# A two-stage kernel on one core: the normalized rows of its second part, turned by VectorE and a trip through DRAM

## The chip, the core and the metric

The kernel runs on one core of a Trainium2 chip. The core has a matrix engine (TensorE, in the profile PE for its matmuls and PEld for its weight loads), VectorE (DVE), ScalarE (ACT), GpSimd (POOL) and SyncE (SP), which here issues the DMAs. Sixteen DMA engines move data between DRAM and the on-chip memory SBUF; matmuls write to PSUM, which has eight banks. The metric is the device time of one execution in microseconds (us). All arithmetic is in float32.

## The reference

Two stages. The first is linear attention with random features; the second mixes its output with a Fourier transform and applies a two-layer network.

```python
def phi(x):
    proj = np.einsum('bhsd,md->bhsm', x, omega)
    sq = np.sum(x * x, axis=-1, keepdims=True) / 2.0
    h = proj - sq
    h = h - np.max(h, axis=-1, keepdims=True)
    return np.exp(h) / np.sqrt(m)
q_p, k_p = (phi(q_s), phi(k_s))
kv = np.einsum('bhsm,bhsd->bhmd', k_p, v)
z = np.sum(k_p, axis=2)
num = np.einsum('bhsm,bhmd->bhsd', q_p, kv)
den = np.einsum('bhsm,bhm->bhs', q_p, z)[..., None] + 1e-06
...
X = np.fft.fft(x, axis=1)
X = np.fft.fft(X, axis=2)
mixed = np.real(X).astype(np.float32)
u = x + mixed
mu = np.mean(u, axis=-1, keepdims=True)
var = np.mean((u - mu) ** 2, axis=-1, keepdims=True)
un = (u - mu) / np.sqrt(var + 1e-06)
ch = np.maximum(un @ w_ch1, 0.0) @ w_ch2
return (u + ch).astype(np.float32)
```

Shapes: q, k and v are 8 x 8 x 576 x 64, so u has 8 x 576 = 4608 rows of 512 numbers; w_ch1 is 512 x 2048 and w_ch2 is 2048 x 512.

## The kernel before

**Two parts.** The first part (to about 424 us) does the attention, the Fourier mixing, which leaves u in a DRAM tensor `us`, and the network for the first 512 rows in four plain tiles of 128. The second part does the network for the other 4096 rows in eight blocks of 512 (`TB`), numbered j = 0 to 7. The change is in the second part.

**One block.** The rows are normalized and turned: `norm_of` (line 966) loads 128 rows of u, VectorE takes mean and variance (`bn_stats`, `bn_aggr`), GpSimd raises the variance to the power -1/2, VectorE subtracts and scales (line 981), TensorE turns the four 128 x 128 squares by transposing them against a unit matrix (line 985), and ScalarE copies the turned tile from PSUM to SBUF (line 989). A matmul needs the contracted index on the partitions, which is why the rows must be turned. `block_norms` (line 1097) does this for the four tiles of a block and leaves two turned halves `un[0]` and `un[1]` of 256 rows each, and forms four sums of their quarters on VectorE (line 1113).

Both matrix products are done by a scheme of the Strassen kind: seven products of half-size instead of eight. `first_of(j, fc)` (line 1240) makes one pair of 128 hidden columns by seven *first products* (line 1252): its moving operand is a quarter of `un` or a sum `tt`, 256 rows wide. ScalarE saves partial results (`s`, line 1266), VectorE adds them with the relu (`hid`, line 1238), GpSimd makes sums of the results (`hs`, line 1319). There are eight such pairs in a block. `product_of(j, i, cells)` (line 1373) makes one of the seven *second products*, each split again in seven parts (*leaves*) of four matmuls (line 1432): 49 leaves a block. Each leaf multiplies by its own 256 KB of prepared second-layer weights, `wl`, which `loads_w2` (line 1327) loads from DRAM ahead of use into a ring of `NWL` buffers. `second_of` (line 1497) loads the rows of u for the residual (`ur`) and stores the results.

**What sets the order.** The order of the instructions on every engine is fixed when the kernel is built. The parts of the work are Python generators that yield a `Step` for each operation, with its engine, an estimated duration, the events it waits for and the buffers it takes and gives. `Listing.run` (line 184) keeps a clock for each engine and always lists the step that can start first by those estimates (`bias` shifts that). So a change of steps changes the order of everything around it. On the chip each engine runs its list in order and waits by semaphores; a waiting instruction holds up all that stands behind it on its engine. SyncE's queue is such a list too. The second part is one call of `Listing.run` (line 1539) over `late_norms`, `halves`, `loads_w2` and `weight_sums`.

Four buffers named `slab` hold `un[0]`, `un[1]` and the sums. There is one set, so the next block's rows can only be turned into place when the first products of this block are done; in the kernel before, the norms of block j + 1 therefore lie among the second products of block j.

Of the kernel before, what the change touches and what calls it, by code (L numbers as in the profile page):

```python
# [17 lines left out]
F32 = mybir.dt.float32  # L18
# [17 lines left out]
PE, ACT, DVE, POOL, SP, NONE = "pe", "act", "dve", "pool", "sp", "none"  # L36
# [244 lines left out]
def kernel(  # L281
# [10 lines left out]
    nc = tc.nc  # L292
# [15 lines left out]
    P = 128  # L308
# [10 lines left out]
    TP = 128  # L319
    NPLAIN = 4  # L320
    TB = 512
    NWL, NSUM = 13, 3
    NTB = (B * S - NPLAIN * TP) // TB
    HF, HT, HM = NFC // 2, TB // 2, DM // 2
    D2, F2 = NDC // 2, DFF // 2
# [621 lines left out]
    def load_rows(dst, t):  # L947
        nc.sync.dma_start(dst, us[P * t : P * (t + 1), :])
# [12 lines left out]
    def events_of(tt):  # L961
        return tuple(sorted({("us", r // S) for t in tt for r in (P * t, P * t + P - 1)}))

    unTs = {}

    def norm_of(j, t, i, pool, dst):

        yield Step(SP, 0.42, 3.0, take=("u",), kb=256)
        u = pool.tile([P, DM], F32, name="u", tag="u", bufs=2)
        load_rows(u[:], t)  # L970
        st = small.tile([P, 6], F32, name="st", tag="st")
        mv = small.tile([P, 2], F32, name="mv", tag="mv")
        rstd = small.tile([P, 1], F32, name="rstd", tag="rstd")
        yield Step(DVE, 1.12 if pool is mlpp else 1.01, bias=-0.23)
        nc.vector.bn_stats(out=st[:], in_=u[:])
        nc.vector.bn_aggr(out=mv[:], in_=st[:])
        nc.vector.tensor_scalar(rstd[:], mv[:, 1:2], 1e-6, None, op0=ALU.add)  # L977
        yield Step(POOL, 1.05 if pool is mlpp else 0.85, port=True, bias=-0.18)
        nc.gpsimd.tensor_tensor(rstd[:], rstd[:], mhalf[:], op=ALU.pow)  # L979
        yield Step(DVE, 0.455, port=True)  # L980
        nc.vector.tensor_scalar(u[:], u[:], mv[:, 0:1], rstd[:], op0=ALU.subtract, op1=ALU.mult)
        yield Step(PE, 0.437, take=("bank",), give=("u",))
        b, tp = got()
        for dc in range(NDC):
            nc.tensor.transpose(  # L985
                tp[:, 128 * dc : 128 * dc + 128], u[:, 128 * dc : 128 * dc + 128], ident[:]
            )
        yield Step(ACT, 0.5, give=(b,), makes=("unT", j, i), bias=0.33)
        nc.scalar.activation(
            out=dst,  # L990
            in_=tp.rearrange("p (d t) -> p d t", d=NDC),
            func=AF.Copy,
        )

# [102 lines left out]
    def block_norms(j, pool):  # L1097
        t0 = (NPLAIN * TP + TB * j) // 128
        yield Step(NONE, take=("slab",) * 4, after=events_of(range(t0, t0 + TB // 128)) + ("converted",))
        un = unTs[j] = [slabs.tile([128, NDC, HT], F32, name="unT2", tag="slab") for _ in range(2)]  # L1100
        tt = [slabs.tile([128, 2, D2, HT], F32, name="tt", tag="slab") for _ in range(2)]
        tts[j] = tt[0][:, 0], tt[0][:, 1], tt[1][:, 0]
        for i in range(TB // 128):
            h, k = divmod(i, HT // 128)
            dst = un[h][:, :, 128 * k : 128 * k + 128]
            yield Fork(norm_of(j, t0 + i, i, pool, dst))
        yield Step(NONE, after=tuple(("unT", j, i) for i in range(TB // 128)), bias=1.54)
        ops = sums_right(
            un[0][:, 0:D2], un[1][:, 0:D2], un[0][:, D2:NDC], un[1][:, D2:NDC], *tts[j]
        )  # L1110
        for i, (o, l, r, op) in enumerate(ops):
            yield Step(DVE, 0.6, makes=("tt", j) if i == 3 else None, port=True, bias=-0.49)
            nc.vector.tensor_tensor(out=o, in0=l, in1=r, op=op)
# [89 lines left out]
    def pairs(start):  # L1203
# [24 lines left out]
    late = ctx.enter_context(tc.tile_pool(name="late", bufs=1))  # L1228
    listing.clock = SECOND
    listing.buffers = {k: [0.0] * n for k, n in dict(  # L1230
        slab=0, u=2, ht=NFC, ur=3, s=6, set=3, wl=NWL, sums=NSUM, part=4,
    ).items()}
    w1s += [late.tile([128, 3, D2, GW], F32, name=f"w1s{g}") for g in range(1, 4)]
    hid = late.tile([128, NFC, TB], F32, name="hid")
# [5 lines left out]
    def first_of(j, fc):  # L1240

        un, tt = unTs[j], tts[j]
        f, f2 = (slice(128 * c, 128 * c + 128) for c in (fc, fc + HF))
        g = 128 * fc // GW
        fg = slice(f.start - GW * g, f.stop - GW * g)
        me = ("first", j, fc)
        lo, hi = hid[:, fc], hid[:, HF + fc]
        t1, t2 = slice(0, HT), slice(HT, TB)

        def product(ps, left, right, start):  # L1250
            for dc in range(D2):
                nc.tensor.matmul(  # L1252
                    ps[:, 0:HT],
                    lhsT=left(dc),
                    rhs=right(dc),
                    start=start and dc == 0,
                    stop=(dc == D2 - 1),
                    skip_group_check=True,
                )

        saved = {}

        def save(name, ps):
            yield Step(ACT, 0.37, 0.1, take=("s",), makes=(me, name), bias=-2.15)
            s = late.tile([128, HT], F32, name="s", tag="s", bufs=6)
            nc.scalar.activation(out=s[:], in_=ps[:, 0:HT], func=AF.Copy)  # L1266
            saved[name] = s

        def added(name, o, ps, with_, give, after=()):
            yield Step(DVE, 0.42, 0.1, after=((me, with_),) + after, makes=(me, name), give=give, bias=1.96)  # L1270
            relu_sum(o, ps[:, 0:HT], saved[with_][:])

        mm = 8 * HT / 1193.0 / 2
        yield Step(PE, mm, after=(("tt", j), ("w1s", g)), take=("bank",), bias=0.37)
        xb, x = got()
        product(x, lambda d: w1[:, d, f], lambda d: un[0][:, d], True)
        yield Fork(save("p1", x))
        yield Step(PE, mm, take=("bank",))
        zb, z = got()
        product(z, lambda d: w1s[g][:, 0, d, fg], lambda d: tt[0][:, d], True)  # L1280
        yield Fork(save("p5", z))
        yield Step(PE, mm, after=((me, "p1"),))
        product(x, lambda d: w1s[g][:, 1, d, fg], lambda d: tt[1][:, d], False)
        yield Fork(save("u2", x))
        yield Step(PE, mm, after=((me, "p5"),), makes=(me, "z"))
        product(z, lambda d: w1s[g][:, 2, d, fg], lambda d: un[1][:, D2 + d], False)
        yield Fork(added("c12", lo[:, t2], z, "u2", (zb, "s"), ((me, "z"),)))
        yield Step(PE, mm, after=((me, "u2"),), makes=(me, "u3"))
        product(
            x,  # L1290
            lambda d: w1s[0][:, 3, d, fg] if g == 0 else w1[:, d, f2],
            lambda d: un[1][:, d],
            False,
        )
        yield Fork(added("c22", hi[:, t2], x, "p5", ("s",), ((me, "u3"),)))
        yield Step(PE, mm, take=("bank",), makes=(me, "y"))
        yb, y = got()
        product(y, lambda d: w1[:, D2 + d, f], lambda d: un[0][:, D2 + d], True)
        yield Fork(added("c11", lo[:, t1], y, "p1", (yb, "s"), ((me, "y"),)))
        last = ("slab",) * 4 if fc == HF - 1 else ()  # L1300
        yield Step(PE, mm, after=((me, "c22"),), give=("set",) + last)
        product(x, lambda d: w1[:, D2 + d, f2], lambda d: tt[2][:, d], False)
        yield Step(ACT, 0.37, 0.1, give=(xb,), makes=(me, "c21"), bias=0.73)
        nc.scalar.activation(out=hi[:, t1], in_=x[:, 0:HT], func=AF.Relu)

        yield Step(
            POOL,
            0.75,
            after=tuple((me, c) for c in ("c11", "c12", "c22"))
            + ((("second", j - 1, ORDER[-1]), "read"),) * (j > 0),  # L1310
            port=True,
        )
        ops = sums_left(
            lo[:, t1], hi[:, t1], lo[:, t2], hi[:, t2], *(hs[:, fc, i] for i in range(3))
        )
        for i, (o, l, r, op) in enumerate(ops):
            if i:
                yield Step(POOL, 0.75, makes=("hs", j, fc) if i == 3 else None, port=True, bias=0.56)
            nc.gpsimd.tensor_tensor(out=o, in0=l, in1=r, op=op)  # L1319
# [204 lines left out]
    def halves():  # L1524
        for j in range(NTB):
            for fc in range(HF):
                yield Step(NONE, take=("set", "ht", "ht"))
                yield Fork(first_of(j, fc))
            cells = {}
            yield Fork(second_of(j, cells))  # L1530
            for i in ORDER:
                yield Step(NONE, take=("set",))
                yield Fork(product_of(j, i, cells))

    def late_norms():
        for j in range(1, NTB):
            yield from block_norms(j, late)

    listing.run([late_norms(), halves(), loads_w2(), weight_sums((1, 2, 3))])


# [28 lines left out]
```

## Time and profile before

| what | value |
|---|---|
| time, median of 3 runs | 1177.97 us (1177.2, 1177.97, 1179.43) |
| span of the profiled execution, first to last instruction | 1180.9 us |
| granted TensorE clock, mean | 0.999 |
| busy PE, DVE, ACT, POOL | 1164.9, 722.6, 452.4, 412.9 us |
| L1252, first products: four groups by operands | 1792 passes of 256 columns |
| L1432, second products: three groups by operands | 3136 passes of 128 columns |
| L985, turning of rows | 144 transposes, 112 of them in the second part |
| moved by DMA | 205.67 MB, mean 174 GB/s |

The profiled execution has no time of its own beside the span; the span is 2.9 us above the median of the runs. A line of the profile names an engine, an operation, the tiles that are written and read, and how often. Each float32 matmul of the program shows as two passes; a transpose shows as one. The mean duration of a pass in the groups overlaps with its neighbours; the pace is read from the chain of waits.

### The profile page before, as it was taken

Reading aid. Unit: us, or ns where it says so; the run is one execution under the profiler, and the core shown is the slowest. Engines: PE = TensorE matmul, PEld = TensorE weight load, DVE = VectorE, ACT = ScalarE, POOL = GpSimd, SP = SyncE. Lnnn points to the kernel's source line nnn. Section 1 sums busy time; section 2 is a strip of 40 time slices with the busy share of each in tenths; the row PEclk is TensorE's granted clock in tenths of the full one; section 3 lists DMA queues with packets and bytes.
Section 4 is the critical chain, followed back from the end, with each engine's and each line's share of the span. In section 5 each row is a group of like instructions: output and inputs, shape, how many; then the busy total and the mean of one; then the engine's idle time right before and its main releaser. Section 6 shows DMA issues by size and latency. Waiting matters only on the chain.

```text
span 1180.9 us, 31428 instructions
## 1 busy us (share of the span) xinstructions
PE 1164.9 (99%) x12549; PEld 1044.6 (88%) x12549; DVE 722.6 (61%) x1552; ACT 452.4 (38%) x1513; POOL 412.9 (35%) x489
## 2 busy tenths in 40 slices
PE   8999999999999999999999999999999999999998
PEld 7878888779787878998998998998999899899898
DVE  7989999976677642762662572473374275266255
ACT  7987888866343212222222222222222222222211
POOL 2443544455462124214314304223322421431421
PEclk9999999999999999999999999999999999999999
DMA  8855756666662260861771582384295095177155
GB/s 238 245 165 173 244 174 180 200 197 178 188 203 91 88 224 10 291 194 52 240 242 64 174 286 85 118 293 134 63 304 179 10 301 193 44 245 236 63 169 189
DMA packets 144705, 205.67 MB, mean 174 GB/s; under 512 B 49072, under 2 KB 58544, under 8 KB 144560
## 3 DMA queue, kind: packets, MB, share of 16 engines
q1 hardware_dynamic: 144064, 203.41, 53.9%
q8 instruction: 99, 1.62, 0.6%
q14 instruction: 46, 0.38, 0.1%
q10 hardware_dynamic: 496, 0.26, 0.1%
HBM read 171.90 MB, written 35.91 MB: 176 GB/s over the span
## 4 chain that ended last, share of the span: by engine, by line
PE 90%; DVE 4%; DMA 3%; ACT 1%; issue 1%; SPq 1%; DVEq 0%; ACTq 0%
PE banks L1252 33%; PE banks L1432 30%; PE banks L1045 5%; PE banks L606 4%; PE banks L1068 4%; PE banks L512 4%; PE banks L640 2%; PE banks L687 2%; DMA kq<-in_q_dram 2%; PE banks L985 2%; PE banks L849 1%; PE banks L799 1%; DVE nmx L549 1%; PE banks L809 1%; DMA kq<-in_k_dram 1%
## 5 line engine op out<-in xcount | busy, mean ns | idle before, releaser
L1238 DVE CUSTOM_DVE_ANT_0 hid<-banks,s 128x256 f32<-128x256 f32 x192 | 79.6, 423 | 255.4 <-PE banks L1252 250.5
L1432 PE MATMUL banks<-wl,sums 128*128 128x128 f32 x1792 | 217.3, 275 | 0.0
L1432 PEld LDWEIGHTS banks<-wl,sums 128*128 128x128 f32 x1792 | 208.8, 192 | 0.4
L566 ACT ACTIVATE e<-banks,nmx 128x128 f32<-128x128 f32 x576 | 164.7, 428 | 24.5 <-DVE nmx L549 24.0
L1266 ACT ACTIVATE s<-banks 128x256 f32<-128x256 f32 x192 | 73.7, 384 | 261.1 <-PE banks L1252 261.1
L1252 PE MATMUL banks<-unT,w 128*128 128x256 f32 x704 | 167.5, 379 | 0.0
L1252 PEld LDWEIGHTS banks<-unT,w 128*128 128x128 f32 x704 | 132.7, 190 | 17.9 <-issue 0.5
L1407 ACT ACTIVATE s<-banks 128x128 f32<-128x128 f32 x168 | 46.6, 278 | 242.3 <-PE banks L1432 195.7
L1252 PE MATMUL banks<-tt,w1s 128*128 128x256 f32 x512 | 126.2, 379 | 0.0
L1319 POOL TENSOR_TENSOR hs<-hid 128x256 f32<-128x256 f32 x64 | 46.4, 725 | 207.9 <-DVE hid L1238 178.9
L1252 PEld LDWEIGHTS banks<-tt,w1s 128*128 128x128 f32 x512 | 97.3, 190 | 13.2
L1412 DVE TENSOR_TENSOR part<-banks,s 128x128 f32<-128x128 f32 x168 | 48.8, 291 | 88.6 <-PE banks L1432 88.4
L549 DVE TENSOR_REDUCE nmx<-banks 128x8 f32<-128x1024 f32 (+1 forms) x96 | 89.3, 951 | 21.6 <-PE banks L606 16.8
L1432 PE MATMUL banks<-wl,hid 128*128 128x128 f32 x768 | 97.6, 275 | 0.0
L1432 PEld LDWEIGHTS banks<-wl,hid 128*128 128x128 f32 x768 | 93.5, 192 | 1.2
L1319 POOL TENSOR_TENSOR hs<-hid,hs 128x256 f32<-128x256 f32 x64 | 46.6, 728 | 119.8 <-issue 94.9
L606 PE MATMUL banks<-om,kqT 64*64 64x128 f32 (+1 forms) x2088 | 80.2, 278 | 2.2 <-ACT kv L656 0.9
L1252 PE MATMUL banks<-unT,w1s 128*128 128x256 f32 x320 | 80.7, 379 | 0.0
L606 PEld LDWEIGHTS banks<-om,kqT 64*64 64x64 f32 (+1 forms) x2088 | 65.4, 140 | 13.8 <-issue 4.4
L979 POOL TENSOR_TENSOR rstd<-rstd,mhalf 128x1 f32<-128x1 f32 x36 | 24.8, 689 | 149.6 <-DVE rstd L977 148.6
L1432 PE MATMUL banks<-wl,hs 128*128 128x128 f32 x576 | 74.9, 275 | 0.4 <-DVE part L1412 0.4
L1432 PEld LDWEIGHTS banks<-wl,hs 128*128 128x128 f32 x576 | 70.0, 192 | 0.9 <-DVE part L1412 0.6
(128 smaller groups left out, 1951.6 us busy)
## 6 DMA issues: line engine op xcount, KB each, us to landing
wl<-w2l SPq DMA_DIRECT2D x392, 256.0 KB, 3.6
raw<-in_moe_w_ch_dram SPq DMA_DIRECT2D x32, 512.0 KB, 5.0
kq<-in_k_dram SPq DMA_DIRECT2D x32, 288.0 KB, 4.4
kq<-in_q_dram SPq DMA_DIRECT2D x32, 288.0 KB, 4.8
vd<-in_v_dram SPq DMA_DIRECT2D x32, 288.0 KB, 4.9
u<-us SPq DMA_DIRECT2D x36, 256.0 KB, 3.9
ur<-us SPq DMA_DIRECT2D x36, 256.0 KB, 3.8
out_dram<-ur SPq DMA_DIRECT2D x34, 256.0 KB, 2.4
```

What stands on the lines that cost most here:

```text
L512: nc.tensor.transpose(ps[:, (j - j0) * 128 : (j - j0 + 1) * 128], src(j), ident[:])
L549: nc.vector.tensor_reduce(nmx[:, :, 0:num], pps[:, :, 0 : MF * num].rearrange("p b (c m) -> p b c m", m=MF), axis=AX.X, op=ALU.max, negate ...
L566: nc.scalar.activation(out=e[:, c + (i if num == 1 else 0), :], in_=pps[:, i, MF * c : MF * c + MF], func=AF.Exp, bias=nmx[:, i, c : c + 1],)
L606: nc.tensor.matmul(pps[cols, c, MF * m : MF * m + MF], lhsT=kqT[rows, j, cols], rhs=om2[rows, :],)
L1045: nc.tensor.matmul(hp[:, 0:TP], lhsT=w1[:, dc, 128 * fc : 128 * fc + 128], rhs=unTs[key][:, dc, :], start=(dc == 0), stop=(dc == NDC - 1),)
L1068: nc.tensor.matmul(yp[:, 0:DM], lhsT=hs[fc][:, 128 * i : 128 * i + 128], rhs=w2[:, fc, :], start=(fc == 0), stop=(fc == NFC - 1),)
L1238: nc.vector._custom_dve(TENSOR_ADD_SAT, out=o, in0=ps, in1=sb, s0=FMAX, s1=0.0)
L1252: nc.tensor.matmul(ps[:, 0:HT], lhsT=left(dc), rhs=right(dc), start=start and dc == 0, stop=(dc == D2 - 1), skip_group_check=True,)
L1266: nc.scalar.activation(out=s[:], in_=ps[:, 0:HT], func=AF.Copy)
L1319: nc.gpsimd.tensor_tensor(out=o, in0=l, in1=r, op=op)
L1412: nc.vector.tensor_tensor(out=part[:, t, 128 * m : 128 * m + 128], in0=ps[:, 0:128], in1=saved[with_][:], op=ALU.add,)
L1432: nc.tensor.matmul(ps[:, 0:128], lhsT=left[:, f], rhs=wls[j, i, n][:, f], start=start and f == 0, stop=(f == 3), skip_group_check=True,)
```

## The change

In blocks 1 to 7 of the second part the rows are no longer turned by TensorE and ScalarE.

- `by_blocks`: VectorE transposes each 32 x 32 square of a normalized tile of 128 rows in place of its position, all 16 squares in one instruction, into a tile `turn` (one buffer). SyncE writes that to a DRAM tensor `turned`, 256 KB in runs of 512 bytes.
- `fetched`: for each half block SyncE reads it back in four DMAs of 128 KB, each into 32 partitions of `un`, so that the squares land where the turned tile needs them. Eight DMAs a block.
- `normed` and `late_turns`: load, statistics, normalization, turn and write are a stream of their own, listed first. It may start for block j once the first pair of columns of block j - 1 has been made; the fetch alone waits for the `slab` buffers.
- The 128 rows of a tile are now taken from two adjacent tiles in alternating groups of 32 (`rows[block[1]]`), so that a run read back is 1 KB.
- `un` and the sums have the layout [row group of 32][piece of 128 features][32 rows] instead of [piece][256 rows]. A first product's moving operand is therefore eight runs of 32 numbers, 128 apart (64 apart in the sums). Block 0 is still turned by TensorE, and ScalarE writes it in the new layout.
- The ring of weights has 12 buffers instead of 13.

```diff
-    NWL, NSUM = 13, 3
+    NWL, NSUM = 12, 3
...
+    Q = 32
+    turned = {}
+
+    def by_blocks(j, i, pool, u, h, k):
+        yield Step(DVE, 0.69, take=("turn",), give=("u",), makes=("turn", j, i))
+        w = pool.tile([P, 4, NDC, Q], F32, name="turn", tag="turn", bufs=1)
+        nc.vector.transpose(
+            out=w[:].rearrange("p g d q -> p d g q"),
+            in_=u[:].rearrange("p (d g q) -> p d g q", d=NDC, g=4),
+        )
+        if (j, h) not in turned:
+            turned[j, h] = dram.tile([P, 4, 2, NDC * Q], F32, name=f"turned{j}_{h}")
+        t = turned[j, h]
+        yield Step(SP, 0.42, 2.6, after=(("turn", j, i),), makes=("turned", j, i), give=("turn",), kb=165)
+        nc.sync.dma_start(t[:, :, k], w[:].rearrange("p g d q -> p g (d q)"))
+
+    def fetched(j, h, dst):
+        yield Step(
+            SP, 1.7, 3.0, after=(("turned", j, 2 * h), ("turned", j, 2 * h + 1)),
+            makes=("unT", j, h), kb=330,
+        )
+        for g in range(4):
+            nc.sync.dma_start(
+                dst[Q * g : Q * g + Q].rearrange("q (b k) d t -> q b (k d t)", k=2),
+                turned[j, h][:, g].rearrange("(b q) k n -> q b (k n)", q=Q),
+            )
+
+    def normed(j, pool):
+        t0 = (NPLAIN * TP + TB * j) // 128
+        yield Step(NONE, after=events_of(range(t0, t0 + TB // 128)) + ((("first", j - 1, 0), "z"),))
+        for i in range(TB // 128):
+            h, k = divmod(i, HT // 128)
+            yield from norm_of(j, t0 + 2 * h, i, pool, None, (h, k))
+
+    def norm_of(j, t, i, pool, dst, block=None):
...
-        load_rows(u[:], t)
+        if block:
+            rows = us[P * t : P * (t + 2), :].rearrange("(b k q) d -> k b q d", k=2, q=Q)
+            nc.sync.dma_start(u[:], rows[block[1]])
+        else:
+            load_rows(u[:], t)
...
+        if block:
+            yield from by_blocks(j, i, pool, u, *block)
+            return
         yield Step(PE, 0.437, take=("bank",), give=("u",))
...
-        un = unTs[j] = [slabs.tile([128, NDC, HT], F32, name="unT2", tag="slab") for _ in range(2)]
-        tt = [slabs.tile([128, 2, D2, HT], F32, name="tt", tag="slab") for _ in range(2)]
+        un = unTs[j] = [slabs.tile([128, HT // Q, NDC, Q], F32, name="unT2", tag="slab") for _ in range(2)]
+        tt = [slabs.tile([128, 2, HT // Q, D2, Q], F32, name="tt", tag="slab") for _ in range(2)]
         tts[j] = tt[0][:, 0], tt[0][:, 1], tt[1][:, 0]
         for i in range(TB // 128):
             h, k = divmod(i, HT // 128)
-            dst = un[h][:, :, 128 * k : 128 * k + 128]
-            yield Fork(norm_of(j, t0 + i, i, pool, dst))
+            if pool is mlpp:
+                dst = un[h][:, 4 * k : 4 * k + 4].rearrange("p g d q -> p d g q")
+                yield Fork(norm_of(j, t0 + i, i, pool, dst))
+            elif not k:
+                yield Fork(fetched(j, h, un[h]))
...
-                    ps[:, 0:HT],
+                    ps[:, 0:HT].rearrange("f (b q) -> f b q", q=Q),
...
-        product(x, lambda d: w1[:, d, f], lambda d: un[0][:, d], True)
+        product(x, lambda d: w1[:, d, f], lambda d: un[0][:, :, d], True)
...
+    def late_turns():
+        for j in range(1, NTB):
+            yield from normed(j, late)
 
-    listing.run([late_norms(), halves(), loads_w2(), weight_sums((1, 2, 3))])
+    listing.run([late_turns(), late_norms(), halves(), loads_w2(), weight_sums((1, 2, 3))])
```

The numbers in the steps are the listing's own estimates; they set the order, not the time.

More of the change, by code (lines that the diff above doesn't have):

```diff
@@ L964 @@
     unTs = {}
-    def norm_of(j, t, i, pool, dst):
+    Q = 32
[29 more added lines that the diff above has]
+    def norm_of(j, t, i, pool, dst, block=None):
         yield Step(SP, 0.42, 3.0, take=("u",), kb=256)
         u = pool.tile([P, DM], F32, name="u", tag="u", bufs=2)
-        load_rows(u[:], t)
+        if block:
[3 more added lines that the diff above has]
+            load_rows(u[:], t)
         st = small.tile([P, 6], F32, name="st", tag="st")
@@ L990, in norm_of @@
             out=dst,
-            in_=tp.rearrange("p (d t) -> p d t", d=NDC),
+            in_=(
+                tp.rearrange("p (d t) -> p d t", d=NDC)
+                if len(dst.shape) == 3
+                else tp.rearrange("p (d g q) -> p d g q", d=NDC, q=Q)
+            ),
             func=AF.Copy,
@@ L1104, in block_norms @@
             h, k = divmod(i, HT // 128)
-            dst = un[h][:, :, 128 * k : 128 * k + 128]
-            yield Fork(norm_of(j, t0 + i, i, pool, dst))
-        yield Step(NONE, after=tuple(("unT", j, i) for i in range(TB // 128)), bias=1.54)
+            if pool is mlpp:
[3 more added lines that the diff above has]
+                yield Fork(fetched(j, h, un[h]))
+        parts = TB // 128 if pool is mlpp else 2
+        yield Step(NONE, after=tuple(("unT", j, i) for i in range(parts)), bias=1.54)
         ops = sums_right(
-            un[0][:, 0:D2], un[1][:, 0:D2], un[0][:, D2:NDC], un[1][:, D2:NDC], *tts[j]
+            un[0][:, :, 0:D2], un[1][:, :, 0:D2], un[0][:, :, D2:NDC], un[1][:, :, D2:NDC], *tts[j]
         )
@@ L1230 @@
     listing.buffers = {k: [0.0] * n for k, n in dict(
-        slab=0, u=2, ht=NFC, ur=3, s=6, set=3, wl=NWL, sums=NSUM, part=4,
+        slab=0, u=2, turn=1, ht=NFC, ur=3, s=6, set=3, wl=NWL, sums=NSUM, part=4,
     ).items()}
@@ L1279, in first_of @@
         zb, z = got()
-        product(z, lambda d: w1s[g][:, 0, d, fg], lambda d: tt[0][:, d], True)
+        product(z, lambda d: w1s[g][:, 0, d, fg], lambda d: tt[0][:, :, d], True)
         yield Fork(save("p5", z))
         yield Step(PE, mm, after=((me, "p1"),))
-        product(x, lambda d: w1s[g][:, 1, d, fg], lambda d: tt[1][:, d], False)
+        product(x, lambda d: w1s[g][:, 1, d, fg], lambda d: tt[1][:, :, d], False)
         yield Fork(save("u2", x))
         yield Step(PE, mm, after=((me, "p5"),), makes=(me, "z"))
-        product(z, lambda d: w1s[g][:, 2, d, fg], lambda d: un[1][:, D2 + d], False)
+        product(z, lambda d: w1s[g][:, 2, d, fg], lambda d: un[1][:, :, D2 + d], False)
         yield Fork(added("c12", lo[:, t2], z, "u2", (zb, "s"), ((me, "z"),)))
@@ L1291, in first_of @@
             lambda d: w1s[0][:, 3, d, fg] if g == 0 else w1[:, d, f2],
-            lambda d: un[1][:, d],
+            lambda d: un[1][:, :, d],
             False,
@@ L1297, in first_of @@
         yb, y = got()
-        product(y, lambda d: w1[:, D2 + d, f], lambda d: un[0][:, D2 + d], True)
+        product(y, lambda d: w1[:, D2 + d, f], lambda d: un[0][:, :, D2 + d], True)
         yield Fork(added("c11", lo[:, t1], y, "p1", (yb, "s"), ((me, "y"),)))
@@ L1301, in first_of @@
         yield Step(PE, mm, after=((me, "c22"),), give=("set",) + last)
-        product(x, lambda d: w1[:, D2 + d, f2], lambda d: tt[2][:, d], False)
+        product(x, lambda d: w1[:, D2 + d, f2], lambda d: tt[2][:, :, d], False)
         yield Step(ACT, 0.37, 0.1, give=(xb,), makes=(me, "c21"), bias=0.73)
```

## The prediction

> **What bounds the kernel now.** I read the page first: who is busy, and at what clock.
>
> ```profile
> span 1180.9 us, 31428 instructions
> PE 1164.9 (99%) x12549; PEld 1044.6 (88%) x12549; DVE 722.6 (61%) x1552; ACT 452.4 (38%) x1513; POOL 412.9 (35%) x489
> PEclk9999999999999999999999999999999999999999
> ```
>
> TensorE (PE) is the bound from end to end at the full granted clock; the other engines have room. A busy PE can still wait, so I read next the chain of waits, in order of time, over one block of the second part (start, length, what):
>
> ```profile
> 748.02 0.89 PE banks L1432 x8
> 748.91 6.05 PE banks L1252 x28
> 754.96 0.89 PE banks L1432 x8
> 755.85 0.86 PE banks L1252 x4
> 756.71 15.19 PE banks L1432 x136
> 771.90 0.93 PE banks L985 x8
> 772.83 16.08 PE banks L1432 x144
> 788.90 0.04 issue
> 788.95 1.11 PE banks L985 x8
> 790.06 8.12 PE banks L1432 x72
> ```
>
> L1252 is a first product, L1432 a second product, L985 the turning of normalized rows. The pieces follow each other without a hole, so a microsecond taken from PE is taken from the end, as long as nothing is late in its place. Each row counts passes; the program's matmul of a product is two of them. A first-product pass costs 6.05/28 = 0.216 us, a second-product pass 16.08/144 = 0.112 us, a leaf of eight 0.893 us. The period is 94.28 us, seven times.
>
> Third, the table by stretch: what the DMA engines do in both halves of the period (last two columns: share, GB/s).
>
> ```profile
> 678.00:690.00 12.00, 12.00 (x110) 12.00 (x110) 8.11 (x18) 3.03 (x9) 3.41 (x4) 1.00 0.93 306
> 728.00:738.00 10.00, 10.00 (x48) 8.81 (x47) 2.55 (x6) 2.11 (x6) 5.74 (x8) 1.00 0.00 1
> ```
>
> During second products the DMA engines are nearly full (each leaf loads 256 KB in 0.893 us); during first products they stand still. Fourth, the groups and the timeline for what a norm costs and for VectorE's free time among first products (in brackets):
>
> ```profile
> L981 DVE TENSOR_SCALAR u<-u,mv,rstd 128x512 f32<-128x512 f32 x28 | 21.2, 778 | 3.1 <-POOL rstd L979 3.1
> L975 DVE BATCH_NORM_STATS2 st<-u 128x6 f32<-128x512 f32 x28 | 19.1, 684 | 0.0
> ```
>
> ```profile
> 676.27 1.50 DVE L981 TENSOR_SCALAR u<-u,mv,rstd 128x512 f32<-128x512 f32 x1 [0.44 <-POOL rstd L979]
> ```
>
> ```profile
> 676.22 2.68 POOL L1472 TENSOR_TENSOR ur<-ur,part 128x512 f32<-128x512 f32 x2
> ```
>
> ```profile
> 728.30 0.42 DVE L1238 CUSTOM_DVE_ANT_0 hid<-banks,s 128x256 f32<-128x256 f32 x1 [4.00 <-PE banks L1252]
> ```
>
> The same L981 takes 0.54 us alone (its median) and 1.50 us while GpSimd (POOL) runs a tensor operation. Last, the transfers, median us from issue to landing:
>
> ```profile
> wl<-w2l SPq DMA_DIRECT2D x392, 256.0 KB, 3.6
> uh<-x SPq DMA_DIRECT2D x16, 256.0 KB, 4.3
> w2l<-big SPq DMA_DIRECT2D x12, 256.0 KB, 2.8
> w2l<-w SPq DMA_DIRECT2D x9, 256.0 KB, 5.8
> ```
>
> The same 256 KB take 2.8 us from 128 partitions in 2 KB runs, 4.3 from 64 partitions, 5.8 in 512-byte runs.
>
> **What the change takes away.** Blocks 1 to 7 lose 16 transposes each. They are the two L985 rows, 0.93 + 1.11 us a period (the second with 0.18 us of waiting for VectorE), all on the chain: 7 x 2.04 = 14.3 us. The order confirms it: between the products of a block no transpose is left, and the counts of both products are unchanged. ScalarE loses 28 evictions of 0.597 us; it is 38% busy, so that is worth nothing.
>
> **The norm moved into the first products.** VectorE runs, per tile, statistics to the normalization's start in 1.98 us (674.29 to 676.27 in the timeline, POOL's power included), the normalization (0.54 to 1.50), and the new 32x32 turn. No row shows such a turn. Bounds for 512 columns: 0.54 (L981, one input, one output) and 0.95 (the reduction L549, mean over 1024 columns); I take 0.68, a 128x512 copy from PSUM (L526). Together 3.1 to 4.4 us, say 3.7, four times a block, in front of the additions L1238 (0.42). By the order, the third chain follows the addition released by one first product and the next addition PE needs is wanted 20 matmuls, 20 x 0.432 = 8.6 us, after that release; VectorE needs 0.42 + 4.4 + 0.42 = 5.2. The fourth: 22 matmuls, 9.5 us, against 6.1. So PE is covered by 3.4 us, and by more at the first two. What can eat the cover is the load of the next rows: SyncE issues it only behind the write of the turned tile, so it lands about 0.8 + 3.9 = 4.7 us after the turn (3.9 is the row of u). Between the third and fourth statistics stand 16 matmuls, 6.9 us, less a chain of 3.7: VectorE waits some 1.5 us for data with two or three additions queued behind, and 1.9 us of cover stay. Cost 0 if the cover holds; each microsecond beyond it costs 7. Bounds 0 and 7; I take 0.7.
>
> **The trip through DRAM.** Turned writes (1 MB a block) and the loads of rows (1 MB) now run among first products, where the share is 0.00: nothing. SyncE's wait for a turn holds back the next load of rows, four loads for the residual, three weight loads of the second set: by the order none of them is used before the second products. In the second products the fetch (eight DMAs, 1 MB) replaces the four row loads that stood there (1 MB): bytes equal.
>
> The order of issue is not equal. Before, two row loads stood between the weights of the second set and those of the third. Now eight fetches do. They are released by the end of the leaf before the last four first-product passes, 0.87 us before the long run of second products (time 0); after one weight issue (0.32) the first goes at about -0.5. An issue costs 0.32 (wl) to 0.61 (uh<-x, three-dimensional). So the first weights of the third set are issued at -0.5 + 8 x 0.32 = 2.1, or at 4.4; they land 2.6 (least, wl) to 4.4 us later: 4.7 to 8.8. By the order the ninth leaf of the run uses them: 8 x 0.893 = 7.1. The loss is 0 to 1.7 us a block, 0 to 12 in all. With 0.45 an issue and a landing of 3.8 they come at 6.9, just in time; because that is so close I put 0.3 a block, 2.1. The loads behind them are used three leaves later or more, by the order, and have that margin.
>
> What the fetch itself takes no row shows. From uh<-x against w2l<-big, half the partitions cost 1.5 us more for 256 KB; the 128 KB stores us<-x, from 64 partitions, land in 2.6 us (median). The fetches are of 128 KB, so I lean on the latter, and the bounds above hold the former. [...]
>
> **The ring of weights** has 12 buffers for 13: loads run 10.7 us ahead at most, and wl lands in 3.6: nothing, while the queue is not blocked as above.
>
> **First products read broken rows.** The moving operand is now eight runs of 32 floats instead of one of 256, in 1792 passes. No row shows such a matmul; bounds: no cost, or what a split write costs ScalarE (L528, 0.445 us for 256 columns in four runs of 64 against 0.384 contiguous in L1266: 16%), 62 us on PE. That row is another engine's and its split side is what it writes, while PE's is what it reads, so I take zero and keep a chance for the rest. The four sums L1113 read runs of 64: L1399, with runs of 128, takes 0.69 against 0.68: nothing.
>
> [...]
>
> **Sum.** 1180.9 - 14.3 + 2.1 + 0.7 = 1169.4 us of span. The median of the three runs is 2.9 below the profiled span, so 1166.5.
>
> **Rivals.**
> - *Late weights.* The third set's first weights come 0.6 to 2.5 us late in each of seven blocks: 1168 to 1181, say 1174. For it: eight issues, half the partitions. Against it: 0.45 us an issue suffices. From 2.04 us a block the change loses.
> - *VectorE late among first products.* Each norm contends with POOL's sums (1.50 against 0.54), the loads slip, PE waits 0.7 to 2 us a block for an addition: 1169 to 1178, say 1171. Against it: a cover of 1.9 us.
> - *The other side: a slower first-product pass.* Place: the 1792 passes of L1252. The gain is gone at 14.3/1792 = 8 ns a pass, 3.7% of 0.216. At 5% it costs 19.4: 1178 - 14.3 + 19.4 = 1183.
> - *The transposes leave and nothing moves*: 1178. Against it: PE has no hole around them.
>
> **How the numbers follow.** Forecast 0.55 (1163.5 to 1169), late weights 0.22 (0.05 of it above 1180), late VectorE 0.09 (0.02 above), slower passes 0.12, no change 0.02. About 0.2% (2.4 us) is what can be told from no change. Faster 0.55 + 0.17 + 0.07 = 0.79; same 0.02; slower 0.05 + 0.02 + 0.12 = 0.19. The range of 8 in 10 leaves out the slower passes and the far ends: 1162.5 to 1178.
>
> **What would show it.** Right: no transpose after the first block; a period near 92.2 us; first-product pieces of 28 passes still 6.05; the turn near 0.68. Wrong, by step: PE waiting for wl<-w2l at the ninth leaf (late weights); PE waiting for L1287 or ScalarE's saves in first products (late VectorE); 28 passes longer than 6.05 (broken rows).

## The result: 1228.9 us, and the profile after

| | before | after |
|---|---|---|
| runs, us | 1177.2 to 1181.2, median 1178.7 | 1221.4, 1227.4, 1230.3, 1232.3, median 1228.9 |
| profiled execution: time, span, us | 1180.9 (span) | 1221.4, span 1219.5 |
| second part, first start of a first product to last start of a second product, us | 423.6 to 1176.3: 752.7 | 418.0 to 1215.1: 797.1 |
| second part against before, us | | +44.4 |

The ratio is 1.041, with a 95% interval of 1.0373 to 1.0447: slower by 50 us where 11.5 fewer were forecast. The profiled execution is the fastest of the four, 7.5 us below the median, and the account below is of that one. The row of the second part, read from the first and last starts of the two matmul lines, is what to compare between kernels: the part ahead of it is not touched by the change, yet ends between 418 and 426 us in the profiles of this study.

The page of the changed kernel, as the first view of before:

```profile
PE 1167.6 (96%) x12437; PEld 1038.9 (85%) x12437; DVE 746.8 (61%) x1573; ACT 436.1 (36%) x1485; POOL 429.1 (35%) x496
```

PE's busy time rose by 2.7 us although 112 transposes left it (12549 instructions became 12437), and its share fell from 99% to 96%: it waits now, and some of its passes have become longer. The chain of waits over one block (start, length, what; L1301 is the first product, L1481 the second, once L1252 and L1432):

```profile
624.16 6.06 PE banks L1301 x28
...
641.55 5.53 DMA u<-us
...
647.11 0.70 DVE st L1013
...
653.12 7.21 issue
...
662.55 1.06 DVE hid L1287 x3
...
663.66 5.41 PE banks L1301 x16
...
669.95 6.05 PE banks L1301 x28
```

The two ends of the stretch are as forecast: no transpose, and 28 passes in 6.05 us. Between them the chain leaves PE for 33 us (PE still works in most of that time; the chain shows what its next release hung on) and runs through the norms: a row load, statistics, GpSimd's power, normalization, and only then the additions L1287 that release PE. The piece of 7.21 us called issue hides another load, as the timeline shows (start, length, engine, instruction; in brackets idle time and what ended it):

```profile
640.21 0.71 DVE L972 STREAM_TRANSPOSE turn<-u 128x512 f32<-128x512 f32 x1
...
640.95 0.54 SPq L980 DMA_DIRECT2D turned<-turn  x1
...
641.55 0.52 SPq L1006 DMA_DIRECT2D u<-us  x1
...
647.11 0.69 DVE L1013 BATCH_NORM_STATS2 st<-u 128x6 f32<-128x512 f32 x1 [4.54 <-DMA u<-us]
...
651.17 0.52 SPq L1006 DMA_DIRECT2D u<-us  x1
...
651.74 2.33 SPq L948 DMA_DIRECT2D ur<-us  x4
...
659.18 0.69 DVE L1013 BATCH_NORM_STATS2 st<-u 128x6 f32<-128x512 f32 x1 [7.67 <-DMA u<-us]
...
663.66 1.44 PE L1301 MATMUL banks<-tt,w 128*128 128x256 f32 x4 [4.71 <-DVE hid L1287]
```

From the end of a turn (640.92) to the next statistics (647.11) it is 6.2 us; before the fourth tile of a block, whose load shares the DMA engines with four loads for the residual, 8.6 (over the seven blocks 5.9 to 7.1, and 7.9 to 8.9 before the fourth tile). A chain of VectorE from statistics to the turn's end is 3.4 (637.48 to 640.92). From the issue of the first row load of the block (619.95) to the end of its fourth turn (662.6) it is 42.7 us, where 168 first-product passes without a hole take 36.3 (1127.8 us, in the last block, which has no norms beside it), and the additions stand behind the norms in VectorE's queue. Over the seven blocks (waiting engine, tile and line, what it waited for: us in all, times, longest):

```profile
DVE st L1013 <- DMA u<-us: 128.3, 28, 7.9
...
PE banks L1301 <- DVE hid L1287: 33.3, 12, 5.0
...
PE banks L1481 <- DMA wl<-w2l: 3.9, 7, 0.7
```

Last, the table by stretch, with the granted clock and the DMA engines' share and GB/s in the last three columns. First what the write and the load of one tile move, then PE's clock around the wait:

```profile
642.00:643.25 1.25, 1.25 (x8) 1.09 (x7) 0.56 (x2) 0.00 (x0) 0.00 (x0) 1.00 0.80 216
643.50:646.00 2.50, 2.50 (x13) 2.21 (x12) 0.00 (x0) 0.77 (x2) 0.00 (x0) 1.00 0.23 84
...
663.60:665.00 1.40, 1.34 (x5) 1.12 (x6) 0.33 (x2) 0.00 (x0) 1.40 (x3) 0.76 0.68 193
665.00:667.00 2.00, 2.00 (x6) 1.58 (x5) 0.06 (x1) 0.38 (x1) 1.92 (x4) 0.50 0.00 0
```

The turned write of 256 KB passes at 216 GB/s and a share of 0.80. The load of the same size behind it runs at 84 GB/s and a share of 0.23, although nothing else moves: 0.23 x 16, about 4 of 16 engines. The packets of the trace say the same: 128 of 2 KB, 84 ns each (median), three or four at a time. And after a wait of 4.7 us PE gets half its clock for 3.4 us (664.34 to 667.75 by the trace's clock records): 16 passes take 5.41 us instead of 3.46.

**The account.** Second part: -14.3 for the transposes, +39.3 of waiting on PE in the seven periods (the holes between its rows; 33.3 of them for additions, 3.9 for weights, 2.1 for the rest), +18.7 of longer passes (busy 664.4 us in seven periods instead of 7 x (94.28 - 2.04)). Together +43.7, and +44.4 is measured. The longer passes are mostly the clock: by the trace's clock records, half the clock was granted once a block, five times for 3.4 us and twice for 6.8, 30.7 us in all. PE worked in some 28 of them, which makes about 14 of the 18.7; the rest was not followed.

### The profile page after: what moved, and what is told of

Read it like the earlier page. It is cut to its first block, busy times and chain, and to the rows that moved or that the text cites. A ratio compares the mean times of both kernels' runs of the same rounds, so it can differ in the third digit from the quotient of the medians.

```text
span 1219.5 us, 31350 instructions
## 1 busy us (share of the span) xinstructions
PE 1167.6 (96%) x12437; PEld 1038.9 (85%) x12437; DVE 746.8 (61%) x1573; ACT 436.1 (36%) x1485; POOL 429.1 (35%) x496
## 4 chain that ended last, share of the span: by engine, by line
PE 71%; DMA 9%; issue 7%; DVE 6%; POOL 4%; ACT 2%; SPq 1%; POOLq 0%; DVEq 0%; ACTq 0%
PE banks L1481 27%; PE banks L1301 16%; DMA u<-us 6%; PE banks L1090 5%; PE banks L606 5%; PE banks L512 4%; PE banks L1113 4%; DMA wl<-w2l 2%; PE banks L640 2%; POOL hs L1368 2%; PE banks L687 2%; PE banks L849 2%; DVE u L1019 1%; PE banks L799 1%; ACT e L566 1%
## 5 line engine op out<-in xcount | busy, mean ns | idle before, releaser
L1481 PE MATMUL banks<-wl,sums 128*128 128x128 f32 x1792 | 217.6, 275 | 0.0
L1481 PEld LDWEIGHTS banks<-wl,sums 128*128 128x128 f32 x1792 | 208.7, 192 | 0.1
L1301 PE MATMUL banks<-unT,w 128*128 128x256 f32 x704 | 172.4, 386 | 5.1 <-DVE hid L1287 3.3
L1301 PEld LDWEIGHTS banks<-unT,w 128*128 128x128 f32 x704 | 136.5, 195 | 25.7 <-DVE hid L1287 3.5
L1287 DVE CUSTOM_DVE_ANT_0 hid<-banks,s 128x256 f32<-128x256 f32 x192 | 72.5, 411 | 124.7 <-PE banks L1301 124.7
L1521 POOL TENSOR_TENSOR ur<-ur,part 128x512 f32<-128x512 f32 x32 | 46.9, 1466 | 267.2 <-ACT part L1514 165.6
L1301 PE MATMUL banks<-tt,w1s 128*128 128x256 f32 x512 | 123.5, 380 | 2.4 <-DVE hid L1287 2.2
L1301 PEld LDWEIGHTS banks<-tt,w1s 128*128 128x128 f32 x512 | 96.4, 190 | 18.1 <-DVE hid L1287 4.8
L1013 DVE BATCH_NORM_STATS2 st<-u 128x6 f32<-128x512 f32 x36 | 24.9, 693 | 134.1 <-DMA u<-us 134.1
L1017 POOL TENSOR_TENSOR rstd<-rstd,mhalf 128x1 f32<-128x1 f32 x36 | 20.5, 569 | 236.1 <-DVE rstd L1015 236.1
L1481 PE MATMUL banks<-wl,hid 128*128 128x128 f32 x768 | 99.6, 276 | 3.9 <-DMA wl<-w2l 3.9
L549 DVE TENSOR_REDUCE nmx<-banks 128x8 f32<-128x1024 f32 (+1 forms) x96 | 89.2, 950 | 17.5 <-PE banks L606 13.2
L1481 PEld LDWEIGHTS banks<-wl,hid 128*128 128x128 f32 x768 | 94.1, 192 | 6.4 <-DMA wl<-w2l 5.2
L1301 PE MATMUL banks<-tt,w 128*128 128x256 f32 x256 | 71.7, 405 | 27.9 <-DVE hid L1287 27.9
L1301 PE MATMUL banks<-unT,w1s 128*128 128x256 f32 x320 | 84.5, 397 | 0.0
L1301 PEld LDWEIGHTS banks<-tt,w 128*128 128x128 f32 x256 | 49.0, 201 | 37.0 <-DVE hid L1287 31.1
L1481 PE MATMUL banks<-wl,hs 128*128 128x128 f32 x576 | 76.3, 275 | 0.4 <-DVE part L1461 0.4
```

The source lines that it names most:

```text
L549: nc.vector.tensor_reduce(nmx[:, :, 0:num], pps[:, :, 0 : MF * num].rearrange("p b (c m) -> p b c m", m=MF), axis=AX.X, op=ALU.max, negate ...
L1287: nc.vector._custom_dve(TENSOR_ADD_SAT, out=o, in0=ps, in1=sb, s0=FMAX, s1=0.0)
L1301: nc.tensor.matmul(ps[:, 0:HT].rearrange("f (b q) -> f b q", q=Q), lhsT=left(dc), rhs=right(dc), start=start and dc == 0, stop=(dc == D2 - 1),
L1481: nc.tensor.matmul(ps[:, 0:128], lhsT=left[:, f], rhs=wls[j, i, n][:, f], start=start and f == 0, stop=(f == 3), skip_group_check=True,)
L1521: eng.tensor_tensor(out=o, in0=o, in1=other, op=ALU.add)
```

## The experiments

The theory: the row load is slow because its DRAM side is four groups of 32 rows, which keeps about 4 engines busy (the share of 0.23), and a norm a block ahead pays that load each time. The rivals: the order on SyncE's queue (the load behind the write behind the turn) whatever the load is split in; and VectorE's own work among first products.

**Four loads of 32 rows.** Nothing else moves on any engine.

```diff
-            nc.sync.dma_start(u[:], rows[block[1]])
+            for b in range(4):
+                nc.sync.dma_start(u[Q * b : Q * b + Q], rows[block[1], b])
```

> The load of a tile's 128 rows is issued as four loads of 32 rows each; every other instruction keeps its place on every engine. Theory (few engines): the changed kernel's load has a DRAM side of 4 groups of 32 rows, only 4 packets of 2 KB are in flight at a time (3.7 us for 128 packets of 84 ns), and four loads of 32 rows each spread over all 16 engines: about 1 us of flow. From the turn's end to the next statistics then some 4.5 us instead of 6.2 to 8.6, in spite of three more issues (3 x 0.33); PE's waits for L1287 (33 us) and the slow passes behind them (16 to 19) go, the late weights (3.9) stay: 1168 to 1177. Rival (order): what delays the statistics is that the load stands behind the turned write on SyncE's queue, whatever it is split in; three more issues make it worse: 1225 to 1235. Rival (VectorE's chain itself, normalization beside GpSimd at 0.95): unchanged, 1221 to 1232.

1173.0 us (1170.8 to 1177.4, six runs), 0.9946 of before (0.9928 to 0.9965); second part 744.8, so 52 us less than in the changed kernel. A trip in its timeline, and its waits:

```profile
621.53 0.71 DVE L972 STREAM_TRANSPOSE turn<-u 128x512 f32<-128x512 f32 x1
...
622.85 2.02 SPq L1007 DMA_DIRECT2D u<-us  x4
626.50 0.70 DVE L1014 BATCH_NORM_STATS2 st<-u 128x6 f32<-128x512 f32 x1 [2.12 <-DMA u<-us]
```

```profile
DVE st L1014 <- DMA u<-us: 35.0, 19, 4.5
...
PE banks L1482 <- DMA wl<-w2l: 5.3, 7, 1.0
```

From the turn's end to the statistics 4.3 us instead of 6.2, with three more issues on the way; from 623.5 to 625.5 the DMA engines have a share of 0.84 and move 226 GB/s, the end of the turned write included. PE's waits for additions are gone. What is left is the late weights, 5.3 us, where the expectation left them at 3.9.

**The dose: two loads of two groups each.**

```diff
-            nc.sync.dma_start(u[:], rows[block[1]])
+            for b in (0, 2):
+                nc.sync.dma_start(u[Q * b : Q * b + 2 * Q], rows[block[1], b : b + 2])
```

> A dose: the same 128 rows loaded as two DMAs whose DRAM side has 2 groups of 32 rows. Theory (few engines: as many as the outermost size of the DRAM side allows): 2 packets in flight, 128 x 84 / 2 = 5.4 us at the least where 4 in flight took 2.7 at the least and 3.7 in the trace; each trip grows by 3 to 4 us, three of them ahead of the last statistics of a block, and PE waits 9 to 12 us longer a block, slow passes behind it not counted: 1290 to 1330. Rival (order, or the chain itself): one more issue a tile (0.5 us, three in a row a block): 1230 to 1245.

1306.6 us, one run, inside the expected 1290 to 1330. The table by stretch during one load, and what PE waited for additions:

```profile
677.00:682.00 5.00, 5.00 (x18) 4.14 (x17) 0.00 (x0) 1.07 (x4) 0.00 (x0) 0.69 0.12 45
```

```profile
PE banks L1302 <- DVE hid L1288: 89.3, 22, 7.7
```

A share of 0.12 and 45 GB/s: about 2 of 16 engines. The trip grows to 9.6 us (11.7 for the fourth tile), and PE waits 89 us for additions instead of 33. Same bytes, same rows, one more issue. By rate and share a busy engine moved some 23 GB/s in both (45/(0.12 x 16) here, 84/(0.23 x 16) in the changed kernel; an estimate), so what differs is how many were busy. Of what was varied here, the number of groups on the DRAM side goes with the speed: 84 GB/s with four, 45 with two.

**Contiguous rows.** The fetch gathers the eight squares from both tiles, in runs of 512 bytes.

```diff
-            rows = us[P * t : P * (t + 2), :].rearrange("(b k q) d -> k b q d", k=2, q=Q)
-            nc.sync.dma_start(u[:], rows[block[1]])
+            load_rows(u[:], t + block[1])
...
-            turned[j, h] = dram.tile([P, 4, 2, NDC * Q], F32, name=f"turned{j}_{h}")
+            turned[j, h] = dram.tile([2, P, 4, NDC * Q], F32, name=f"turned{j}_{h}")
...
-        nc.sync.dma_start(t[:, :, k], w[:].rearrange("p g d q -> p g (d q)"))
+        nc.sync.dma_start(t[k], w[:].rearrange("p g d q -> p g (d q)"))
...
-                dst[Q * g : Q * g + Q].rearrange("q (b k) d t -> q b (k d t)", k=2),
-                turned[j, h][:, g].rearrange("(b q) k n -> q b (k n)", q=Q),
+                dst[Q * g : Q * g + Q].rearrange("q b d t -> q b (d t)"),
+                turned[j, h][:, :, g].rearrange("k (b q) n -> q (k b) n", q=Q),
```

> Contiguous rows: a tile takes 128 rows in one piece, its turned write is contiguous (2 KB a partition instead of four runs of 512 bytes), and the fetch reads eight runs of 512 bytes a partition instead of four of 1 KB. All orders on all engines as in the changed kernel. Theory (few engines): as with four loads, but with one issue (0.3 us) a tile: from the turn's end to the next statistics about 3.6 us; PE's waits for L1287 go; the fetch carries twice the packets (27 ns against 46), which adds 0 to 0.6 us to the late weights a block: 1166 to 1177. Rival (order): 1219 to 1230.

1174.5 us (1173.2 to 1177.6, seven runs), 0.9956 (0.9943 to 0.9969); second part 748.6. The table by stretch during one load, which is a single DMA as in the changed kernel:

```profile
626.30:627.80 1.50, 1.50 (x9) 1.30 (x8) 0.37 (x1) 0.38 (x1) 0.00 (x0) 1.00 0.94 303
```

128 rows on the DRAM side: a share of 0.94 and 303 GB/s, against 0.23 and 84 with four groups and 0.12 and 45 with two. From the turn's end to the statistics two of three trips in a block mostly take 3.2 to 3.6 us, as expected; in the other the rows are there before VectorE has done the additions ahead. No wait for additions is left on PE either; the weights now come late by 8.6 us in all, 1.2 a block, 0.5 a block more than with four loads. The fetch's shorter packets are the likely reason, since its eight issues are the same.

**Loads ahead, still of four groups.** The loads of a block are a stream of their own, listed as soon as a buffer is free.

```diff
+    def row_loads(j, t0, pool, rowtiles):
+        for i in range(TB // 128):
+            t, k = t0 + i // 2 * 2, i % 2
+            yield Step(SP, 0.42, 3.0, take=("u",), kb=256, makes=("row", j, i))
+            u = rowtiles[i] = pool.tile([P, DM], F32, name="u", tag="u", bufs=2)
+            rows = us[P * t : P * (t + 2), :].rearrange("(b k q) d -> k b q d", k=2, q=Q)
+            nc.sync.dma_start(u[:], rows[k])
...
+        rowtiles = {}
+        yield Fork(row_loads(j, t0, pool, rowtiles))
```

> The load stays as it is (4 groups of 32 rows in one DMA), but the four loads of a block are a stream of their own: the load of tile i+2 is listed ahead of the turned write of tile i, as soon as its buffer is free. If the serial trip (turn, write, load, statistics) is what costs, whichever part of it is slow, the load now lies beside the chain of the tile between: the statistics of the third tile come about 6 us after the first turn, with 3.4 us of the second chain in that time, so VectorE waits some 2.5 us once a block instead of 6 to 9 three times: PE's waits go nearly all, 1168 to 1180. Rival (the normalization beside GpSimd and the turn are too much work for VectorE among first products): the waits stay, 1215 to 1232.

1175.8 us (1173.7 to 1176.3, six runs), 0.9962 (0.9949 to 0.9975); second part 747.4. VectorE waits 13.2 us for rows instead of 128.3. So the slow load costs only because it stands in series with the turn: give it more of the engines (the share of 0.84 with four loads, 0.94 with contiguous rows), or something to hide behind, and the loss is gone. Of the rivals, VectorE's own work is out as the cause: it does the same chains here in time. The order alone is out as the cause of the slow load, and in as the condition under which it costs.

**The fetch split.** Four of the eight fetches wait for the end of set 2, on top of the four loads.

```diff
-            SP, 1.7, 3.0, after=(("turned", j, 2 * h), ("turned", j, 2 * h + 1)),
+            SP, 1.7, 3.0,
+            after=(("turned", j, 2 * h), ("turned", j, 2 * h + 1)) + ((("second", j - 1, 2), "read"),) * h,
```

> Four loads of 32 rows as before, and the fetch of the second half (four of the eight DMAs) waits for the end of the second product's last leaf of set 2, so that it is issued behind 14 weight loads instead of ahead of them. With all eight fetches in a row PE waited 0.5 to 1.0 us for wl<-w2l once a block (5.3 us in all). Theory (issue): the wait is the time that SyncE needs to issue eight fetches (3.7 us) ahead of the third set's weights; with four of them the weights are issued 1.9 us earlier and come in time, and the later four meet a full ring: 1167 to 1170. Rival (bytes): the fetched 1 MB takes DMA time that the weights lack, wherever it stands; the wait moves to a later leaf: 1172 to 1176.

1165.7 us (1164.7 to 1169.3, five runs), 1.3 below the expected range, 0.9878 of before (0.9861 to 0.9895); second part 738.4, that is 14.3 below before. Its chain over a block, and its only wait for weights:

```profile
611.00 36.26 PE banks L1303 x168
...
655.96 41.09 PE banks L1483 x368
```

```profile
PE banks L1483 <- DMA wl<-w2l: 0.3, 1, 0.3
```

No hole is left there: 168 first-product passes in 36.26 us, 368 second-product passes in 41.09. The same 1 MB is fetched, so the rival that its bytes cost wherever they stand is out. That the issues alone were the cause isn't shown, because the split takes both issues and bytes from ahead of the weights. In the changed kernel both stand there (the eight fetches, then the weights, and the stretch in which the fetches pass):

```profile
677.29 3.74 SPq L988 DMA_DIRECT2D unT<-turned  x8
681.13 8.41 SPq L1384 DMA_DIRECT2D wl<-w2l  x12
```

```profile
678.75:683.50 4.75, 4.75 (x45) 4.75 (x44) 4.75 (x9) 1.11 (x4) 1.41 (x2) 1.00 1.01 235
```

The weights are issued behind 3.74 us of issues, and then wait while the DMA engines are full with the fetches (share 1.01): PE gets them at 685.36. With plain rows the same eight issues cost more (8.6 us instead of 5.3), which speaks for the bytes as a part of it.

**Split fetch with the loads ahead as well.** Both edits as above.

> The same split of the fetch, four loads of 32 rows, and the row loads as a stream of their own ahead of the turned writes. Theory: with 16 engines a tile's load no longer holds anything back, so listing it ahead adds nothing: the same as with the split alone within 2 us, 1167 to 1170. Rival: a remaining cost of VectorE's waits for u<-us (35 us idle in the run with four loads, none of it seen on PE) shows: 2 to 4 us faster than the split alone.

1170.5 us (1167.7 to 1171.4, five runs), 0.991 (0.9896 to 0.9924): not the same within 2 us as expected, and not faster, but 4.9 slower than the split alone. Its second part is 741.9, 3.5 longer, with 3.5 us of waiting on PE where the split alone has 0.7, nearly all in the second products of the first block; another 2.1 lies ahead of the second part, where the two kernels do the same. Listing the loads ahead moves instructions on every engine; why the first block suffers was not followed further.

**Split fetch with contiguous rows.** Both edits as above.

> Contiguous rows and contiguous turned writes (as in the run with plain rows) together with the split fetch; orders on TensorE and VectorE as in the run with four loads and the split fetch. Theory: with the fetch split the late weights go here too (8.6 us in the run with plain rows, 1.2 us a block, where the fetch takes twice the packets), so it ends at or a little below the split with four loads: 1163 to 1168. Rival (packets of 512 bytes take the DMA time that the weights lack): part of the 8.6 us stays on other leaves: 1169 to 1174.

1166.6 us (1164.2 to 1167.3, five runs), 0.9893 (0.9876 to 0.991), second part 739.3. The 8.6 us of late weights fall to 0.6. It can't be told from the split with four loads.

**Not a block ahead.** Four loads, eight fetches in a row, and the norms released by the last first product of the block before.

```diff
-        yield Step(NONE, after=events_of(range(t0, t0 + TB // 128)) + ((("first", j - 1, 0), "z"),))
+        yield Step(NONE, after=events_of(range(t0, t0 + TB // 128)) + ((("first", j - 1, HF - 1), "z"),))
```

> Four loads of 32 rows, eight fetches in a row, but the norms of a block start behind the last first product of the block before instead of its first one: they stand among second products, a block ahead no more. Theory (room on the DMA engines): in 36 to 44 us of second products the weights need 12.5 MB, and row loads, turned writes and fetches add 3 MB instead of 1; at the 306 GB/s of that stretch 15.5 MB take 51 us, and the ring's lead covers about 7: PE waits 0 to 5 us a block for wl<-w2l: 1175 to 1208. Rival (what counts is only that the load has its 16 engines, the place is free): 1170 to 1176.

1270.4 us (1262.6 to 1275.9, four runs), 1.0756 (1.0715 to 1.0796): beyond both expectations. The first stretch of second products in one block, and two waits:

```profile
583.80:605.00 21.20, 14.97 (x123) 14.06 (x121) 10.60 (x22) 2.88 (x10) 4.12 (x5) 0.94 0.67 211
```

```profile
PE banks L1482 <- DVE hid L1288: 30.9, 7, 5.4
...
PE banks L1482 <- DMA wl<-w2l: 23.7, 26, 3.0
```

The sign of the theory held, its mechanism did not: in the stretch with the longest wait the DMA engines have a share of 0.67 on average, so they are not what is short. By the chain of waits the last additions of the first products stand behind a norm that waits for its rows, and weights stand on SyncE's queue behind a turned write that waits for that norm; PE waits for both in turn, and pays the lower clock (0.94 in this stretch) on top. That reading rests on this one profile; no run separates the two waits. What it does show is that the place matters: the same norms with the same loads cost 97 us less a block ahead.

## Why the prediction was wrong, point by point

- **The failed step** is in the norm's cover: "SyncE issues it only behind the write of the turned tile, so it lands about 0.8 + 3.9 = 4.7 us after the turn (3.9 is the row of u)". The serial path was right, the 3.9 was the row of another load: 128 contiguous rows, which moved at a share of 0.94 where a trace shows them alone (the run with contiguous rows). The change reads four groups of 32 (share 0.23), and the trip took 6.2 to 8.6 us. With four loads it is 4.3 in the trip shown, so 4.7 was the price of a load that the changed kernel does not issue. The cover of 1.9 us was used up by the third tile. The price set on this, 0.7, was 33.3 of waiting. The prediction also put the bytes that move among first products at nothing; the fourth tile's load, beside four loads for the residual, took some 2 us longer.
- **A term that was missing**: the clock. Around one wait of 3.3 to 5.0 us in each block it fell to half (0.50) for 3.4 us, in two blocks for 6.8, which makes about 14 of the 18.7 us of longer passes; these are a third of the 58.0 us lost (39.3 + 18.7).
- **The rival "VectorE late among first products"** named the place and the wait (PE for L1287) but took 0.7 to 2 us a block; it was 4.8, and with the longer passes up to 7.4. A chance of 0.09 was too little for a cover that hung on one row.
- **The transposes**: 14.3 forecast, and 14.3 is what the second part gains once nothing is late (752.7 to 738.4); with contiguous rows it gains 13.4 (739.3), so the agreement to the tenth is luck.
- **The chain on VectorE**: 3.7 forecast, 3.4 measured. The turn is 0.711 us against 0.68. Normalization is 0.94 beside GpSimd, within the bounds of 0.54 and 1.50. The bound of 0.95 from the reduction L549 was a misreading, the mean over two shapes (1.217 for 1024 columns, 0.419 for 256); nothing hung on it.
- **Late weights**: the right place, 0.3 a block forecast, 0.56 measured (3.9 over seven). Eight issues took 3.74 us, 0.47 each (forecast 0.45), and the weights landed 4.2 us behind their issue (forecast 3.8). With the fetch split 0.3 is left in all. How much was issue and how much the bytes of the fetch stays open.
- **Fetches to 32 partitions**: no row of before had such a transfer, and the landing of 3.8 us in the sum was the author's estimate between 2.6 and 4.4. From 678.75 to 683.50 of the changed kernel's trace 235 GB/s passed at a share of 1.01, slower than the 306 of the second products before; but several fetches were in flight at once, so no run shows what one reaches alone. With the fetch split PE waits 0.3 us for weights in all.
- **Broken rows for PE**: zero forecast, zero measured (28 passes in 6.05, 168 in 36.26). **The ring of 12**: with the fetch split 0.3 us of waiting for weights is left with it.
- **The sum**: 1166.5 was forecast, and the two kernels with fast loads and a split fetch take 1165.7 and 1166.6, but that is partly luck. They hardly pay the 2.8 us that the sum held for late weights and norms (PE waits 0.7 and 1.1 us in their second parts), and the kernel before took 1180.5 and 1179.4 beside them instead of 1178.0: they gain 14.8 and 12.9, where 14.3 was forecast for the transposes alone. The fairer test is the change with nothing but its load mended: it gains 6.7 (1179.7 to 1173.0) where 11.5 was forecast, and the late weights, 5.3 instead of 2.1, are most of the difference.

What would have priced the load came only with the runs: shares of 0.23 with four groups, 0.12 with two and 0.94 with 128 rows, which by share x 16 is about 3.7, 1.9 and 15 busy engines. The prediction's own question to the profile, who else waits behind a late load, was the right one; it was asked with the wrong duration.

## What to carry to other kernels

When an edit changes a transfer's pattern, look at the outermost size of its DRAM side before taking a row of the same tile as its price: 256 KB in 4 groups moved at 84 GB/s, in 2 groups at 45, in 128 rows at 303. A load that stands in series with the work that frees its buffer must be priced as a trip, from the last use to the next, times its number in the stage, and set against that stage. Where a queue feeds an engine that is never idle, spread a burst of transfers: four fetches instead of eight in a row were worth 6.4 us of the second part (744.8 to 738.4).

## What was not expected of the hardware

- After PE had waited 4.7 us, its granted clock was 0.76, then 0.50 from 665 to 667 us, and full again before 669. A wait of 1.25 us (at 649.66) left the passes behind it at their length. In the second part of the changed kernel the clock records show half the clock around all seven waits of 3.26 to 4.96 us and around none of the others, which are of 1.87 us and less. In the run that is not a block ahead it went with a wait of 2.67 us too (until 622.07): 14 second-product passes from 623.06 took 3.16 us, where 14 x 0.112 are 1.6, and the mean clock from 622 to 641 was 0.91.
- A VectorE turn in 32x32 squares of 128x512 takes 0.711 us in all 28 cases, writing runs of 32 floats, little more than the statistics of the same tile (0.69).
- A moving operand in eight runs of 128 bytes costs TensorE nothing that 1792 passes show: their median is 379 ns before and after, and with the split fetch none is above 383.
